# Second channel layer in seven block products for some rounds, and a new order at the seams between batches

## The chip, the cores and the metric

One core of a Trainium2 chip. The metric is the device time of one execution in microseconds (us), taken as the median over runs. A core has a matrix engine (TensorE, PE in the profile, with its weight loads listed apart as PEld), a vector engine (VectorE, DVE), a scalar engine (ScalarE, ACT), a general engine (GpSimd, POOL) and a sync engine that issues transfers (SyncE, SP). Each engine works through its own queue of instructions in order, and waits at an instruction until what it needs is there. All data are 32-bit floats in on-chip memory (SBUF, 128 partitions); TensorE writes to a small accumulator memory (PSUM), from which VectorE and ScalarE read.

## The reference

Block-sparse attention, its output laid out as B x S x 512, then a block of a Fourier mix, a normalization and two channel layers. B = 4, H = 8, S = 768, D = 64, w_ch1 is 512 x 2048 and w_ch2 2048 x 512.

```python
scores = np.where(mask, q @ k.T / sqrt(D), -1e9)          # mask: blocks of 32 x 32
attn = softmax(scores) @ v                                # (B, H, S, D) -> x: (B, S, H*D)
...
mixed = np.real(fft(fft(x, axis=1), axis=2))
u = x + mixed
un = (u - mean(u)) / sqrt(var(u) + 1e-6)                  # along the last axis
out = u + np.maximum(un @ w_ch1, 0.0) @ w_ch2
```

## The kernel before

**Attention.** The heads of a batch go in four pairs. A unit is 128 keys by 384 queries of a pair; a slot is two units, a pair has six slots and a batch 24. For a unit TensorE makes the scores s (`scores`, L578), ScalarE their exponentials (`weigh`), and TensorE the values o (`values`, L652). The block mask comes in one of two ways. Where a unit is in `by_pe`, TensorE adds a large negative number to the masked scores by a product of two small bf16 `factors` (L588), and ScalarE writes the exponentials straight to a tile e (L598). Else ScalarE exponentiates in place (L606) and VectorE multiplies with a 0/1 mask (L608). Sums over the keys are gathered on POOL (`gather`, L638), or on VectorE (L633). Tiles e come from a pool `ep` of four.

**Placing.** A finished half of a pair's values, oT, is put into x (two tiles, xA and xB, for the halves of the sequence; each has two buffers, so batch b writes where batch b-2 was and has to wait until that one is stored). `place` turns oT on TensorE (xt, L675) and copies it by ScalarE (L676). For later pairs `place_blocks` (L686) does it by 16 transfers of 12 KB each, SBUF to SBUF (L691).

**Mixer.** It runs on x of batch b while the attention of the next batches goes on. `norm_steps` scales x by the reciprocal sums (L761); fold steps (128x1536, L784), along steps and across steps (pq, L887 on) make the Fourier mix; arrive and spread add it to x and take its statistics; `whiten` (L951) makes un. In batches 0 to 2 un is turned by blocks on VectorE and through DRAM (`un_blocks` L1010, far<-un; `un_back` L1020, unT<-far, eight transfers); in the last by TensorE (utp, L992).

**Channel layers.** The first layer is `quad` (L1077): two 128-wide blocks of its outputs by seven block products in place of eight (Strassen's way with fewer sums), each 2 matmuls of 128x384. What they need are sums of blocks of unT (`right`, L1052) and of weights (`left`, L1065 to L1072). VectorE adds the products up (L1095), ScalarE does the relu (L1099). The second layer is `channels` (L1142): for one half and one block m of 128 tokens, four matmuls of 128x512 (L1146) and an add into x (L1149). A round r is quads 2r and 2r+1 and then six calls of `channels`; a batch has four rounds, after the last of which x is stored (`store`, L1157). The last batch's second layer (`outputs`) is already in seven block products of four 128x256 matmuls (L1211).

**Order.** It is written out when the program is built. `slot(sl)` issues a slot of attention. The mixer's steps wait in a queue `apart`, quads and channel calls in `late`, placings and sums of the attention in `short`. `gap` issues steps of `apart` and `short` that fit by reckoned clocks (`when`, one for each engine, and `state["ready"]`); `until(met)` issues channel steps, each with a gap behind it, until a condition holds, such as that a half of batch b-2 is stored (`finished`). `begin(b)` starts a mixer, and from its last step on (`go`) units are masked by VectorE. Constants reckon waits: `BACK` is the time until unT is back, `LEAVES` the time from the last store's issue until x is free. At a seam, where batch b-2 has to be stored ahead of the placing of the first pair of batch b, `slot` calls `until` and then puts the placing into `short`, due after `LEAVES`.

Of the kernel before, what the change touches and what calls it, by code (L numbers as in the profile page):

```python
# [99 lines left out]
def kernel(  # L100
# [14 lines left out]
    nc = tc.nc  # L115
# [61 lines left out]
    ep = ctx.enter_context(tc.tile_pool(name="ep", bufs=4))  # L177
    acc_p = ctx.enter_context(tc.tile_pool(name="acc_p", bufs=2))
    sum_p = ctx.enter_context(tc.tile_pool(name="sum_p", bufs=1))
    big = ctx.enter_context(tc.tile_pool(name="big", bufs=1))  # L180
    tr_p = ctx.enter_context(tc.tile_pool(name="tr_p", bufs=2))
    zc_p = ctx.enter_context(tc.tile_pool(name="zc_p", bufs=1))
# [502 lines left out]

    def place_blocks(n, half):  # L686
        b, j = pairs[n]
        oT = o_of.pop((n, half)).rearrange("p (c t d) -> p c t d", t=P // BLK, d=BLK)
        for g in range(P // BLK):
            for t in range(P // BLK):  # L690
                nc.sync.dma_start(  # L691
                    out=x_of[b, half][BLK * t:BLK * t + BLK, :, j * P + BLK * g:j * P + BLK * (g + 1)],
                    in_=oT[BLK * g:BLK * g + BLK, :, t, :])

    def into_sums(key, j, sp):
        if j == 0:
# [281 lines left out]
    def mixer(b, xA, xB):  # L978
# [34 lines left out]
        def un_back():  # L1013

            for half in range(2):
                unT[half] = tr_p.tile([P, ND, T * P], FP32, tag="tr", name="unT")
                of = lines[half].rearrange("m (g j) (k a i) -> a j k (m g) i",
                                           j=BLK, a=P // BLK, i=BLK)
                for a in range(P // BLK):
                    nc.sync.dma_start(  # L1020
                        out=unT[half][BLK * a:BLK * a + BLK].rearrange(
                            "j k (g i) -> j k g i", i=BLK),
                        in_=of[a])
            state["back"] = max(when["PE"], state["ready"]) + BACK[b > 0]

        t, s = {}, {}
        K1, K2 = slice(0, ND // 2), slice(ND // 2, ND)
# [49 lines left out]
        def quad(p):  # L1077

            g = p // 2 % 2 if last else 0
            if p % 2 == 0:  # L1080
                for i in range(2):
                    hs[g, i] = room((2, 0)[g] + i, [P, 4, HS], "h" + "AB"[i])
            l1, l2 = 2 * (p % 2), 2 * (p % 2) + 1
            h11, h12, h21, h22 = (hs[g, i][:, l, :] for l in (l1, l2) for i in range(2))
            a11, a12, s2, a22 = blocks(p)
            b11, b21, b22 = unT[0][:, K1, :], unT[0][:, K2, :], unT[1][:, K2, :]

            def product(to, a, c, after=0.0):
                for k in range(ND // 2):
                    nc.tensor.matmul(to, a[:, k, :], c[:, k, :], start=(k == 0),  # L1090
                                     stop=(k == ND // 2 - 1))
                return busy("PE", PRODUCT, after) + HOP

            def plus(to, ps, a, at):
                tt(out=to, in0=ps, in1=a, op=ALU.add)  # L1095
                return busy("DVE", SUM, at) + HOP

            def relu(h, at):
                nc.scalar.activation(out=h, in_=h, func=ACT.Relu)  # L1099
                busy("ACT", RELU, at)  # L1100

            def combine(j):
                left(p + 1, j)
                busy("DVE", COMBINE)

            x, at = ps_m.tile([P, 512], FP32, tag="m", name="xp")[:, 0:HS], bank("m")
            z5, z7 = (ps_s.tile([P, 2, 512], FP32, tag="s", name=name)[:, 0, 0:HS]
                      for name in ("z5", "z7"))
            done = product(x, a11, b11)
            nc.scalar.copy(out=h11, in_=x)  # L1110
            p1 = busy("ACT", RELU, done) + HOP
            give(at, p1 - HOP)
            y, at = ps_m.tile([P, 512], FP32, tag="m", name="yp")[:, 0:HS], bank("m")
            p2 = product(y, a12, b21)
            done = product(z7, s2, t[2])
            u2 = plus(h21, z7, h11, max(done, p1))
            c11 = plus(h11, y, h11, p2)
            relu(h11, c11)
            done = product(z5, s[1], t[1])
            plus(h12, z5, h21, done)  # L1120
            combine(1)
            done = product(z7, s[3], t[3], u2)
            u3 = plus(h21, z7, h21, done)
            c22 = plus(h22, z5, h21, done)
            z_at[0] = c22
            relu(h22, c22)
            combine(3)
            gap(0.0, 1.9)
            done = product(y, a22, t[4], c11)
            c21 = plus(h21, y, h21, done)  # L1130
            give(at, c21 - HOP)
            relu(h21, c21)
            gap(0.0, 1.9, "t")
            done = product(z7, s[4], b22, u3)
            z_at[1] = plus(h12, z7, h12, done)
            relu(h12, z_at[1])
            combine(4)
            if last:
                for j in ((1, 2), (3, 4))[p % 2]:
                    output_right(p // 4, j, p // 2 % 2)  # L1140

        def channels(r, half, m):  # L1142

            y, at = ps_m.tile([P, DM], FP32, tag="m", name="y"), bank("m")
            for l in range(4):
                nc.tensor.matmul(y, hs[0, half][:, l, m * P:(m + 1) * P], w2_sb[:, 4 * r + l, :],  # L1146
                                 start=(l == 0), stop=(l == 3))
            x = (xA, xB)[half]
            nc.vector.tensor_tensor(out=x[:, m, :], in0=y, in1=x[:, m, :], op=ALU.add)  # L1149
            give(at, busy("DVE", 0.7, busy("PE", 3.45) + HOP))  # L1150
            if r == NF // 4 - 1:
                store(half, m)

        def store(half, m, cols=slice(0, DM), queue=nc.sync):
            x = (xA, xB)[half]
            for p0, cnt, rows in _rows(out[b][:, cols], T * half + m):
                queue.dma_start(out=rows, in_=x[p0:p0 + cnt, m, cols])  # L1157
            if m == out_of[half][-1]:
                finished.add((b, half))

        last = b == B - 1
        OUT = (2, 0, 1)
        out_of = (OUT, OUT if last else (0, 1, 2))
# [111 lines left out]
        if not last:  # L1278
# [3 lines left out]
                              sp[1][1], wh[0][0], ft[0][0], sp[1][2], wh[1][1], ft[1][1],  # L1282
                              sp[1][0], wh[1][2], ft[1][2], wh[1][0], ft[1][0]]
            after = ([("-", un_back, 0.0, 0.0, 0.0)] + le +
                     [("b", lambda i=i: right(i, 0, 1, 2), 0.0, 0.0, 1.0) for i in (1, 2, 3, 4)])
        rest = []
        for r in range(2 if last else 0):
            rest += [(lambda p=p: quad(p), 7 * PRODUCT) for p in range(4 * r, 4 * r + 4)]
# [2 lines left out]
        for r in range(0 if last else NF // 4):  # L1291
# [9 lines left out]
    MOST, LEAST = 9.6, 2.5  # L1301
    COVER = 100.0
    AHEAD = 2.2
    BACK = 13.0, 12.0
    ALONE = 3.0
    LEAVES = 9.0
    SP = UP // SLOT
    SB = SP * NP
    W_PACE = 1.42
# [1 line left out]
    asked = set()  # L1311
    needed = set()
    state = {"paired": False, "total": None, "w": 0, "got": 0, "owed": 0.0, "ready": 0.0,
             "back": 0.0}

    def channel_step():
        late.popleft()[0]()

    def behind(kind):

        at = max(when["DVE"], state["ready"])
        return 0.75 * (len(kind) - 1) if when["POOL"] > at else 0.0

    def do_apart():
        kind, fn, pe, act, dve, _ = apart.popleft()
        if kind[0] in "dwb":
            dve += behind(kind)
            state["ready"] = busy("DVE", dve, {"w": rstd_at[0] if rstd_at else 0.0,
                                               "b": state["back"]}.get(kind, state["ready"])) + HOP
            fn()  # L1330
            return
# [10 lines left out]
            give(at, done - HOP)  # L1342
        state["ready"] = done

    def gap(rest=0.0, ahead=None, kinds="tm"):

        used = "".join(k for k in "tm" if k not in kinds)
        if ahead is None:
# [1 line left out]
        while apart:  # L1350
# [3 lines left out]
            if kind[0] in "dwb":  # L1354
                dve += behind(kind)
                if kind in "wb" and (state["back"] if kind == "b" else rstd_at[0]) > max(
                        when["DVE"], when["PE"]) + 0.2:
                    break
                if max(when["DVE"], state["ready"]) + dve > when["PE"] + rest + ahead:
                    break  # L1360
            elif kind != "-":
                bank_at = max(min(free[k]) for k in kind)
# [9 lines left out]
                short.remove(item)  # L1372
                fn()

    def until(met):

        while not met():
            if late:
                channel_step()
                gap(2.0)  # L1380
            else:
                do_apart()

    def begin(b):

# [6 lines left out]

        def go():
            late.extend(rest)
            masks["by_pe"] = False
        apart.append(("-", go, 0.0, 0.0, 0.0, hold))

    def rest():
# [19 lines left out]
    def slot(sl):  # L1418
# [28 lines left out]
            keep_mask = mask_step(2 * (sl // 3 - 1) + sl % 3 // 2)  # L1447
        for u, ps in got:
            weigh(u, ps)
        if keep_mask:  # L1450
            keep_mask()
        if BY_VECTOR <= n + 1 < len(pairs):
# [12 lines left out]
        if s == 0 and 0 < n < len(pairs) - 1:  # L1465
            load_k(n + 1)

        reuse = n % NP == 0 and phase >= 2
        if s >= (5 if reuse else 3) and (n, 0) in oT_at and once(n):
            b, j = pairs[n]  # L1470
            at = oT_at[n, 0]
            if reuse:
                until(lambda: (b - 2, 0) in finished)
                at = when["PE"] + LEAVES
            if in_blocks(n):
                place_blocks(n, 0)
            else:
                short.append(("t", at, lambda: place(n, 0)))
# [44 lines left out]
        for _ in range(4 if phase > 1 and not late and len(apart) < 6 * T else 0):  # L1523
            if apart and not late and (apart[0][0] != "b" or
                                       state["back"] < max(when["DVE"], when["PE"]) + 0.2):
                do_apart()

        must = (3, 5) if paired else (2, 5)
        soon = r == 0 and all(i[1] < when["PE"] + 1.0 for i in short)
# [47 lines left out]
        if sl == B * SB - 2:  # L1577
            over = nc.values_load(flag[0:1, 0:1], min_val=0, max_val=1)
    begin(B - 1)
    until(lambda: len(finished) == 2 * B)  # L1580
    ordered.close()


# [102 lines left out]
```

## Time and profile before

| | |
|---|---|
| runs, median (lowest to highest) | 1059.56 us (1056.76 to 1062.27), 3 runs |
| the profiled execution | 1059.17 us, of which the span 1057.5 us |
| TensorE clock, mean over the span | 0.993 of full |
| TensorE: s L578, o L652 | 155.2 us, 142.7 us |
| TensorE: y L1146 (hB, hA) | 129.2 us, 127.9 us |
| TensorE: z L1090 by unT, t | 93.1 us |
| POOL: sums of attention L638 | 163.6 + 47.1 us |

The span is the time between the first and last instruction of the profiled execution. A group in the profile is named by line, engine, operation and its tiles: out<-in. Busy times of groups on TensorE overlap at their ends, since matmuls are pipelined. Two instructions appear in the trace for each 32-bit matmul (two passes). Idle time is given with its releaser: the instruction whose end let the waiting one go.

### The profile page before, as it was taken

How to read it: one execution, taken by the hardware profiler on the slowest of the kernel's cores; microseconds unless marked ns; L12 is line 12 of the kernel's file. 1: busy time of each engine (PE TensorE's matmuls, PEld its weight loads, DVE VectorE, ACT ScalarE, POOL GpSimd, SP SyncE). 2: the span in 40 equal slices, each digit the busy share in tenths (PEclk: the TensorE clock that was granted, in tenths of full speed). 3: DMA queues.
4: the chain of work that ended last, by engine and by line, in shares of the span. 5: the costliest groups of instructions: out<-in, count | busy, mean ns of one | idle time of the engine just before them, and what ended most of it. 6: DMA issues, size and time to landing. Idle time of an engine off the chain costs nothing.

```text
span 1057.5 us, 12421 instructions
## 1 busy us (share of the span) xinstructions
PE 1022.8 (97%) x4338; PEld 530.7 (50%) x4338; DVE 675.3 (64%) x1235; ACT 356.2 (34%) x718; POOL 240.2 (23%) x270
## 2 busy tenths in 40 slices
PE   8989999997999999999999999899999999999996
PEld 4434345433465553444444654444444654578585
DVE  5899795968745744564578467565457364674663
ACT  6988755562020111342441212153220211210210
POOL 1000183565000100454553001256520001000000
PEclk9999999999999999999999999999999999999998
DMA  7757422292000124212230003821000001000001
GB/s 210 228 177 227 107 47 46 50 140 36 1 0 21 40 30 76 62 32 50 41 56 1 1 10 93 107 39 27 11 11 6 0 1 38 23 1 1 1 17 46
DMA packets 160385, 55.71 MB, mean 53 GB/s; under 512 B 145708, under 2 KB 151098, under 8 KB 160314
## 3 DMA queue, kind: packets, MB, share of 16 engines
q1 hardware_dynamic: 159062, 54.10, 23.9%
q10 hardware_dynamic: 1220, 0.72, 0.3%
q8 instruction: 36, 0.59, 0.2%
q14 instruction: 35, 0.29, 0.1%
q0 software_dynamic: 32, 0.01, 0.0%
HBM read 41.44 MB, written 11.01 MB: 50 GB/s over the span
## 4 chain that ended last, share of the span: by engine, by line
PE 82%; DVE 8%; ACT 3%; DMA 3%; issue 2%; SPq 1%; ACTq 0%; DVEq 0%
PE y L1146 23%; PE z L1090 15%; PE s L578 10%; PE o L652 9%; PE yp L1090 7%; PE yy L1211 7%; PE xp L1090 4%; PE zp L856 2%; ACT e L598 1%; DMA out_dram<-x 1%; PE sp L719 1%; PE s L588 1%; DVE t L1052 1%; DVE x L926 1%; DVE acc L633 1%
## 5 line engine op out<-in xcount | busy, mean ns | idle before, releaser
L638 POOL TENSOR_TENSOR acc<-acc,e 128x384 f32<-128x384 f32 x162 | 163.6, 1046 | 103.8 <-DVE e L608 84.5
L578 PE MATMUL s<-qT,kT 64*128 64x384 f32 x768 | 155.2, 518 | 13.0 <-DVE e L608 6.5
L652 PE MATMUL o<-e,vr 128*64 128x384 f32 x768 | 142.7, 499 | 0.0
L1146 PE MATMUL y<-w_sb,hB 128*128 128x512 f32 x288 | 129.2, 600 | 0.3 <-DVE x L1149 0.3
L1146 PE MATMUL y<-w_sb,hA 128*128 128x512 f32 x288 | 127.9, 595 | 0.0
L1149 DVE TENSOR_TENSOR x<-y,x 128x512 f32<-128x512 f32 x72 | 49.7, 691 | 119.9 <-PE y L1146 119.8
L608 DVE TENSOR_TENSOR e<-s,mask 128x768 f32<-128x768 f32 x90 | 82.0, 951 | 54.9 <-ACT s L606 47.6
L578 PEld LDWEIGHTS s<-qT,kT 64*128 64x128 f32 x768 | 63.8, 186 | 92.3 <-ACT e L598 25.2
L638 POOL TENSOR_TENSOR acc<-e 128x384 f32<-128x384 f32 x42 | 47.1, 1143 | 254.5 <-ACT e L598 124.6
L606 ACT ACTIVATE s<-s 128x768 f32<-128x768 f32 x90 | 68.4, 792 | 89.4 <-PE s L578 89.1
L1090 PE MATMUL z<-unT,t 128*128 128x384 f32 x256 | 93.1, 486 | 2.0 <-DVE hA L1095 2.0
L598 ACT ACTIVATE e<-s 128x768 f32<-128x768 f32 x102 | 77.7, 811 | 48.5 <-PE s L588 32.0
L1146 PEld LDWEIGHTS y<-w_sb,hB 128*128 128x128 f32 x288 | 53.9, 192 | 67.6 <-issue 65.8
L1146 PEld LDWEIGHTS y<-w_sb,hA 128*128 128x128 f32 x288 | 53.7, 190 | 63.7 <-issue 60.2
L652 PEld LDWEIGHTS o<-e,vr 128*64 128x64 f32 x768 | 48.2, 137 | 71.6 <-issue 68.7
L1095 DVE TENSOR_TENSOR hA<-z,hA 128x384 f32<-128x384 f32 x64 | 35.7, 558 | 69.8 <-PE z L1090 69.6
L1099 ACT ACTIVATE hA<-hA 128x384 f32<-128x384 f32 x64 | 33.5, 523 | 129.3 <-DVE hA L1095 129.3
L1090 PEld LDWEIGHTS z<-unT,t 128*128 128x128 f32 x256 | 48.6, 190 | 36.8 <-DVE hA L1095 3.1
L1099 ACT ACTIVATE hB<-hB 128x384 f32<-128x384 f32 x64 | 33.5, 523 | 86.6 <-DVE hB L1095 86.6
L1110 ACT COPY hA<-xp 128x384 f32<-128x384 f32 x32 | 15.3, 478 | 116.0 <-PE xp L1090 116.0
L1090 PE MATMUL z<-t,w_sb 128*128 128x384 f32 x128 | 46.9, 489 | 5.0 <-DVE e L608 3.4
L1090 PE MATMUL z<-t,t 128*128 128x384 f32 x128 | 47.8, 497 | 0.0
(208 smaller groups left out, 1367.0 us busy)
## 6 DMA issues: line engine op xcount, KB each, us to landing
wraw<-in_moe_w_ch_dram SPq DMA_DIRECT2D x32, 512.0 KB
vr<-in_v_dram SPq DMA_DIRECT2D x30, 192.0 KB
far<-un SPq DMA_DIRECT2D x18, 256.0 KB
unT<-far SPq DMA_DIRECT2D x24, 192.0 KB
qb<-in_q_dram SPq DMA_DIRECT2D x44, 96.0 KB
kb<-in_k_dram SPq DMA_DIRECT2D x44, 96.0 KB
x<-oT SPq DMA_DIRECT2D x192, 12.0 KB
out_dram<-x SPq DMA_DIRECT2D x11, 252.0 KB
```

The lines of the kernel that those rows point to most:

```text
L578: nc.tensor.matmul(s[:, i, 0:HS], kT[rows, c * P:(c + 1) * P], qT[rows, queries], start=True, stop=u not in by_pe)
L598: nc.scalar.activation(out=e, in_=s[:, :, 0:HS], func=ACT.Exp, scale=scale)
L606: nc.scalar.activation(out=s[:, :, 0:HS], in_=s[:, :, 0:HS], func=ACT.Exp, scale=scale)
L608: nc.vector.tensor_tensor(out=e, in0=s[:, :, 0:HS], in1=m.broadcast_to([P, 2, HS]), op=ALU.mult)
L638: nc.gpsimd.tensor_add(out=acc[:, i, :], in0=start[:, i, :], in1=e[:, i, :])
L652: nc.tensor.matmul(o[D * i:D * i + D, :], vt[:, i, c, :], e[:, i, :], start=(c == 0), stop=(c == C - 1))
L1090: nc.tensor.matmul(to, a[:, k, :], c[:, k, :], start=(k == 0), stop=(k == ND // 2 - 1))
L1095: tt(out=to, in0=ps, in1=a, op=ALU.add)
L1099: nc.scalar.activation(out=h, in_=h, func=ACT.Relu)
L1146: nc.tensor.matmul(y, hs[0, half][:, l, m * P:(m + 1) * P], w2_sb[:, 4 * r + l, :], start=(l == 0), stop=(l == 3))
L1149: nc.vector.tensor_tensor(out=x[:, m, :], in0=y, in1=x[:, m, :], op=ALU.add)
L1211: nc.tensor.matmul(ps, a[:, k, :], c[k // 2][:, k % 2, :] if isinstance(c, list) else c[:, k, :], start=(k == 0), stop=(k == 3))
```

## The change

1. **Rounds in seven products.** Where a quad with an even number is issued while `until` runs with `alone` set, and the round isn't the batch's last, the round's second layer goes by `round_of`: for each m, one 2 x 2 product of blocks (token halves by halves of the round's hidden units, and these by halves of the 512 outputs) in seven products of two matmuls of 128x256. In the order as built these are five rounds: 0, 1 and 2 of batch 0, 2 of batch 1 and 2 of batch 2. The sums of weights are made by POOL (`round_right`), those of hidden values by VectorE (1 and 2) and POOL (3 and 4) (`round_left`). Products go into x by VectorE from PSUM (`plus`, and `both` for two at once), or are copied out by ScalarE (`keep`) and added by POOL (`later`). The sums' room is the four e tiles and a new one; `drain` first issues the values that still need e.
2. **Placing by blocks** goes through DRAM: four transfers out and four back in place of 16.
3. **Seams.** The first placing of a pair that reuses x is issued behind the exponentials of the next slot, not when due by `LEAVES`. `until` runs one slot earlier there if there are late steps, `LEAVES` is 13 (9), `BACK` of batch 2 is 15 (12), the rights of batch 0 are reckoned at 1.7 (1.0), POOL's hindrance (`behind`) at 0.25 in rounds alone (0.75). Masking by VectorE starts with the first channel step, not with `go`. A pending total is issued once the batch before is stored, ahead of a mixer step on PSUM. `gap` can be given a start (`start`) by which alone steps on VectorE are let in. A half counts as stored after three full stores. The last `until` runs with `alone`.

The diff, cut to its core:

```diff
     def place_blocks(n, half):
         b, j = pairs[n]
-        oT = o_of.pop((n, half)).rearrange("p (c t d) -> p c t d", t=P // BLK, d=BLK)
+        rows = far_p.tile([BLK, T, P // BLK, P], FP32, tag=f"oT{half}", name="row", bufs=2)
+        oT = o_of.pop((n, half))
         for g in range(P // BLK):
-            for t in range(P // BLK):
-                nc.sync.dma_start(
-                    out=x_of[b, half][BLK * t:BLK * t + BLK, :, j * P + BLK * g:j * P + BLK * (g + 1)],
-                    in_=oT[BLK * g:BLK * g + BLK, :, t, :])
+            nc.sync.dma_start(
+                out=rows.rearrange("r c t f -> r (c t) f")[:, :, BLK * g:BLK * g + BLK],
+                in_=oT[BLK * g:BLK * g + BLK, :].rearrange("r (ct d) -> r ct d", d=BLK))
+        for t in range(P // BLK):
+            nc.sync.dma_start(
+                out=x_of[b, half][BLK * t:BLK * t + BLK, :, j * P:(j + 1) * P],
+                in_=rows[:, :, t, :])
...
+            if not last:
+                if p % 2 == 0:
+                    seven[p // 2] = state["alone"] and p // 2 < NF // 4 - 1
+                elif seven[p // 2]:
+                    state["drain"]()
+                    sums_room()
+                    for j in (1, 2, 4, 3):
+                        round_right(p // 2, j)
...
+        def round_right(r, j):
+            a, c = {1: (part(r, 0, 1), part(r, 0, 0)), 2: (part(r, 1, 1), w_t[1]),
+                    3: (part(r, 1, 1), part(r, 0, 1)), 4: (part(r, 1, 0), w_t[2])}[j]
+            nc.gpsimd.tensor_tensor(out=w_t[j], in0=a, in1=c, op=ALU.subtract)
...
+        def round_left(m, j):
+            a11, a12, a21, a22 = tokens(m)
+            to, a, c, op = {1: (h_s[1], a21, a22, ALU.add), 2: (a21, h_s[1], a11, ALU.subtract),
+                            3: (h_s[3], a22, a21, ALU.subtract),
+                            4: (h_s[4], a12, a21, ALU.subtract)}[j]
+            if j > 2:
+                nc.gpsimd.tensor_tensor(out=to, in0=a, in1=c, op=op)
...
+            else:
+                tt(out=to, in0=a, in1=c, op=op)
...
+            if m == OUT[0]:
+                round_left(m, 1)
+                round_left(m, 2)
+            c_at, at = ps_m.tile([P, 512], FP32, tag="m", name="yc")[:, 0:DH], bank("m")
+            a_at = plus(a0, c_at, product(c_at, a12, part(r, 1, 0), True))
+            give(at, a_at - HOP)
+            k0 = keep(0, u_at, product(u_at, a11, part(r, 0, 0), True, z_at[0]))
+            later(a0, 0, max(a_at, k0))
+            o_at, at = ps_m.tile([P, 512], FP32, tag="m", name="yc")[:, 0:DH], bank("m")
+            give(at, plus(b0, o_at, product(o_at, a22, w_t[4], True)) - HOP)
+            if m == OUT[0]:
+                round_left(m, 3)
+                round_left(m, 4)
+            gap(start=0.9)
+            k1 = keep(1, u_at, product(u_at, a21, w_t[2], False, k0))
+            later(a1, 1, k1)
+            k2 = keep(2, d_at, product(d_at, h_s[1], w_t[1], True, z_at[1]))
+            done = product(u_at, h_s[3], w_t[3], False, k1)
+            tt(out=both, in0=both,
+               in1=u_at.rearrange("p (o d) -> p o d", o=1).broadcast_to([P, 2, DH]), op=ALU.add)
+            z_at[0] = busy("DVE", 0.7, done) + HOP
+            later(b1, 2, max(z_at[0], k2))
+            z_at[1] = plus(a1, d_at, product(d_at, h_s[4], part(r, 1, 1), False, k2))
+            ahead(1, 2, 3, 4)
+            state["soon"] = 1.6
...
             after = ([("-", un_back, 0.0, 0.0, 0.0)] + le +
-                     [("b", lambda i=i: right(i, 0, 1, 2), 0.0, 0.0, 1.0) for i in (1, 2, 3, 4)])
+                     [("b", lambda i=i: right(i, 0, 1, 2), 0.0, 0.0, 1.0 if b else 1.7)
+                      for i in (1, 2, 3, 4)])
...
     def channel_step():
+        masks["by_pe"] = False
         late.popleft()[0]()
...
     def do_apart():
         kind, fn, pe, act, dve, _ = apart.popleft()
+        if finished and kind[0] in "mt" and state["total"] in short:
+            short.remove(state["total"])
+            state["total"][2]()
...
-                if max(when["DVE"], state["ready"]) + dve > when["PE"] + rest + ahead:
+                at = max(when["DVE"], state["ready"]) - when["PE"]
+                if at + dve > rest + ahead if start is None else at > start:
                     break
...
         for u, ps in got:
             weigh(u, ps)
+        if state["place"]:
+            state["place"]()
+            state["place"] = None
...
-        if s >= (5 if reuse else 3) and (n, 0) in oT_at and once(n):
+        if s >= ((4 if late else 5) if reuse else 3) and (n, 0) in oT_at and once(n):
             b, j = pairs[n]
             at = oT_at[n, 0]
             if reuse:
-                until(lambda: (b - 2, 0) in finished)
-                at = when["PE"] + LEAVES
-            if in_blocks(n):
+                until(lambda: (b - 2, 0) in finished, s == 4)
+                state["place"] = lambda: place(n, 0)
+            elif in_blocks(n):
                 place_blocks(n, 0)
```

Beside `round_of`, `plus` is a VectorE add of 128x256 from PSUM into x, `keep` a ScalarE copy of 128x256 out of PSUM, `later` a POOL add of it into x, `ahead` the lefts of the next m.

## The prediction

> **What bounds the kernel now.** First the page's busy rows, the tenths by slice and the granted clock, then the chain that ended last: is one engine the limit, and everywhere?
>
> ```profile
> PE 1022.8 (97%) x4338; PEld 530.7 (50%) x4338; DVE 675.3 (64%) x1235; ACT 356.2 (34%) x718; POOL 240.2 (23%) x270
> ...
> PE   8989999997999999999999999899999999999996
> ...
> PEclk9999999999999999999999999999999999999998
> ...
> PE 82%; DVE 8%; ACT 3%; DMA 3%; issue 2%; SPq 1%; ACTq 0%; DVEq 0%
> ```
>
> TensorE is busy for 1022.8 of 1057.5 us, so time can come from two places only: fewer passes through it, or the 34.7 us in which it stands. The slices below 9 tell where it stands; the stretches there, with the clock in the third column from the right, are these (us, then busy time and count of PE, PEld, DVE, ACT, POOL; clock; DMA share; GB/s):
>
> ```profile
> 234.00:262.00 28.00, 22.65 (x91) 10.32 (x87) 22.92 (x29) 11.21 (x24) 15.30 (x14) 0.94 0.45 53
> 260.00:400.00 140.00, 140.00 (x428) 75.96 (x427) 81.96 (x168) 23.36 (x51) 11.84 (x20) 1.00 0.11 20
> 405.60:420.00 14.40, 12.44 (x49) 4.87 (x51) 8.18 (x10) 4.68 (x8) 0.00 (x0) 0.88 0.35 73
> 672.00:695.00 23.00, 17.71 (x72) 8.18 (x72) 13.12 (x19) 7.04 (x17) 5.50 (x7) 0.93 0.37 80
> ```
>
> In the channel rounds alone (260 to 400) TensorE never stands. At the three seams, where a batch's rounds begin or end, it loses 5.35, 1.96 and 5.29 us and some clock besides: 28 x 0.06 = 1.7, 14.4 x 0.12 = 1.7, 23 x 0.07 = 1.6 us. Its timeline says behind what (brackets: idle before, and what ended it):
>
> ```profile
> 245.19 1.61 PE L1090 MATMUL z<-t,w_sb 128*128 128x384 f32 x4 [3.36 <-DVE e L608]
> ...
> 251.35 1.56 PE L1090 MATMUL z<-unT,t 128*128 128x384 f32 x4 [1.99 <-DVE hA L1095]
> ...
> 412.73 2.35 PE L578 MATMUL s<-qT,kT 64*128 64x384 f32 x8 [1.96 <-DVE e L608]
> ...
> 674.43 1.53 PE L1090 MATMUL z<-t,w_sb 128*128 128x384 f32 x4 [1.58 <-DVE t L1052]
> ...
> 689.37 2.50 PE L578 MATMUL s<-qT,kT 64*128 64x384 f32 x8 [3.71 <-DVE e L608]
> ```
>
> And why the exponentials' products (e, L608) were late is in ScalarE's timeline:
>
> ```profile
> 410.51 0.48 ACT L676 COPY x<-xt 128x384 f32<-128x384 f32 x1 [13.10 <-DMA out_dram<-x]
> 410.88 1.50 ACT L606 ACTIVATE s<-s 128x768 f32<-128x768 f32 x2
> ...
> 687.09 0.48 ACT L676 COPY x<-xt 128x384 f32<-128x384 f32 x1 [4.82 <-DMA out_dram<-x]
> 687.46 1.50 ACT L606 ACTIVATE s<-s 128x768 f32<-128x768 f32 x2
> ```
>
> The placing copy (L676) needs x free, so it waits for the store of two batches earlier, and the exponentials stand in ScalarE's queue behind it.
>
> **The rounds.** Pass prices come from two runs of equal passes:
>
> ```profile
> 564.78 10.46 PE L1146 MATMUL y<-w_sb,hB 128*128 128x512 f32 x24
> 575.08 1.45 PE L1090 MATMUL xp<-unT,w_sb 128*128 128x384 f32 x4
> ...
> 945.45 3.62 PE L1211 MATMUL yy<-ot,os 128*128 128x256 f32 x16
> 948.90 1.89 PE L1211 MATMUL yy<-w_sb,os 128*128 128x256 f32 x8
> ```
>
> 24 passes of 512 columns take 575.08 - 564.78 = 10.30, 0.429 each; 16 of 256 take 948.90 - 945.45 = 3.45, 0.2156 each. A matmul is two passes. A round was 48 x 0.429 = 20.60; as seven products of two matmuls for each of three blocks it is 84 x 0.2156 = 18.11. Gain 2.49; five rounds **-12.45**. Weight loads (190 ns in group L1146) stay under 215.6.
>
> What else a round costs. VectorE: six adds of 0.69 go; in come six lefts and nine adds of 128x256 (0.42 each, as L1218 and L1072 show) and three adds of 128x512 (0.69): 8.4 for 4.1 in 18.1 us. ScalarE: nine 128x256 copies, 0.38 each by a 128x257 one. Both fit. POOL has no 128x256 row; its 128x384 add takes 0.965 alone (four in 3.87 at 440.53) and 1.23 beside VectorE (eight in 9.83 at 233.62), hence an estimate of 0.64 to 0.82, and 1.29 to 1.64 for 128x512. The four factors of weights (5.2 to 6.6) lie under the second quad (7 products, about 9 us). In the block, one product is 4 x 0.2156 = 0.86. VectorE's second left is ready some 2.2 after the start, needed at 2.59. POOL's lefts 3 and 4 stand behind its first add: ready at 4.2 to 4.5 and 4.9 to 5.3, needed at 4.31 and 5.17: 0 to 0.5 lost in each first block; later blocks have theirs made ahead, 0 to 0.3. Bounds 0 to 8 (the upper under the second rival); I take **+2.0**, nearer the lower, since VectorE is free for some 10 us of a round.
>
> Here a rule speaks against the change. Row: a VectorE 128x768 subtract of two SBUF operands takes 0.95 at 406.87 with POOL idle and up to 1.75 at 240.86 beside it. The Trainium skill, "SBUF — State Buffer", section "Who interferes with whom", says such an instruction and a GpSimd one that reads SBUF exclude each other, the second blocked wholly. The trace agrees in part: 1.75 is less than 0.95 plus a whole 1.23. By it the sum becomes the second rival's.
>
> Four more units are masked on TensorE (L588): 4 passes take 186.94 - 186.52 = 0.42 a slot, two slots **+0.84**.
>
> **Seam A (238 to 252).** The first quad's products wait because the mask products (L608) and four slow rights (1.63 to 1.75 each) share VectorE. After, both slots before the quad are masked on TensorE, so their exponentials need no VectorE, and the quad starts near 242 rather than 245. The five x<-x,r (4.43 from 246.40), which made the 1.99, start later, since a total is taken early and steps are spread. -(5.35 + 1.7) + 0.5 left = **-6.55** (bounds -7.05 to 0).
>
> **Seam B (405 to 420).** The placing is issued behind the next slot's exponentials, so they no longer wait for the store; transposes and copy stand behind them, needed only by later mixer steps. -(1.96 + 1.7) + 0.5 = **-3.2** (-3.7 to 0).
>
> **Seam C (655 to 695).** The same for 3.71, and stores now go out before the unT loads on SP's queue, which made both copy and rights late; but eight unT transfers (issued 657 to 668, landed near 672) still come under 6 us before their use. I leave 2.0: -(1.58 + 3.71 + 1.6) + 2.0 = **-4.9** (-6.9 to 0).
>
> **Seam D (876 to 905).** The last batch's first rounds now start with the across steps behind them: after p8 VectorE has about 10 us of steps before the next transposes, with 20 us of TensorE work as cover, but utp and the first z follow in one run. Idle there was 0.35 + 0.80 + 0.25 = 1.4; by my layout 3.4: **+2.0** (0 to +4).
>
> **Attention behind B and C** runs 7 to 8 slots without channel work in place of 4. A slot is 2.83 us on TensorE, and POOL's sums 2 units x 5/6 x 1.93 = 3.22: 0.4 a slot for up to seven slots, 0 to 2.7 each; the first slots have slack in the e tiles: **+1.5**.
>
> **Placing by blocks**: 16 transfers cost SP 10.32 us (445.35); after, 4 + 4 with a landing between, 2.6 + 2.8 (a store's DMA) + 2.6 = 8. SP's next are loads a pair ahead; the one consumer that waited (x, L761, 3.1 us) is hidden by TensorE work. **0** (-1 to +3, the 3.1 if the cover is gone).
>
> The changed reckonings (BACK, LEAVES, `right`, `behind`) and the count of stores issue nothing; they shift steps, and what that does is in the terms of the seams.
>
> **Sum**: -12.45 + 2.0 + 0.84 - 6.55 - 3.2 - 4.9 + 2.0 + 1.5 = -20.8; 1059.17 - 20.8 = **1038**. The profiled 1059.17 (span 1057.5, 1.67 around it) is 0.4 under the median 1059.56, which I neglect.
>
> **Rivals.**
>
> 1. *The seams' waits come back at the rights.* Seams A and C have a second releaser, the rights (L1052) and, for C, the landing of unT; exponentials that are early gain nothing there. Back come 3.36 + 1.7 at A and 1.58 + 1.71 + 1.6 at C: 1038 + 10 = **1048**. For it: t L1052 ended the 1.58. Against: at A the rights end at 244.2 only because mask products and POOL's eight sums lie beside them. Chance 0.18.
> 2. *POOL shuts out VectorE in the rounds.* Each of the first two lefts waits for a whole POOL instruction, 0.75: 2.2 + 1.5 - 2.59 = 1.1 in five first blocks, 0.3 in ten later ones, 8.5 in place of 2.0: **1045**. For it: 1.75 beside 0.95. Against: adds with a PSUM operand (hA L1095) take 0.56 either way. Chance 0.13.
> 3. *Slower: long mixer steps queued on VectorE between a round's adds.* In the three rounds of batch 0 they are there: sa and sd folds (128x1536, L784, 1.75 to 1.85 alone; x 1.75/0.95 beside POOL = 3.2). A block gives 0.8 of slack, so each such step stops TensorE for 2.4, as the adds hold the two PSUM tiles that the next block opens with. In all 15 blocks 36 us in place of 2: 1038 + 34 = **1072**. It decides from (20.8 + 2)/15 = 1.5 us a block. Against: the trace has eight such folds in all, and x<-x,r at 0.89 fits the slack. Chance 0.12.
> 4. *No new waits at all*: without the terms +2.0, +2.0, +1.5 and the 3.0 left at the seams, **1030**. Chance 0.07.
>
> That the rounds aren't split where they are said to be is not a rival: seven products are chosen while a batch's rounds run alone, which is known when the program is laid out.
>
> **How the numbers follow.** Forecast 0.50 (own range 1033 to 1044), rivals 0.18, 0.13, 0.12, 0.07. No change means within 0.5% of 1059.56, 1054.3 to 1064.9, about what a measurement can tell. Faster: 0.50 + 0.07, 0.15 of rival 1, 0.11 of rival 2 = 0.83. Same: 0.03 + 0.02 + 0.03 of rival 3 = 0.08. Slower: the 0.09 left of rival 3. The range goes from rival 4, 1030, to 1055, past rivals 1 and 2 with the upper bounds of D and of the attention stretches (+2 and +4).
>
> **What would show it.** Rounds: 14 passes of 256 columns in a row start 0.216 apart, with under 0.5 us idle in a first block; waits there for POOL's lefts speak for my term, for VectorE's lefts for rival 2, for x adds behind folds for rival 3. Seam A: no idle over 1 us at the first z; B: L606 ahead of L676 in ScalarE's timeline and no dip in the clock; C: idle of at most 2 in all. A sum under 1055 with idle left at L1052 is rival 1. The forecast is wrong if TensorE stands more than 25 us in all or its passes are slower than 0.22.

## The result, and the profile after

| | median of runs (lowest to highest) | profiled span | clock |
|---|---|---|---|
| before | 1059.47 us (1056.71 to 1062.27), 20 runs | 1057.5 us | 0.993 |
| after | 1061.2 us (1059.8 to 1063.49), 20 runs | 1060.2 us | 0.986 |

The ratio is 1.0022, with a 95% interval of 1.0013 to 1.0030: a little slower, where 1038 us was forecast. Some 23 us of expected gain are missing. The page after, in the same rows:

```profile
PE 1014.9 (96%) x4526; PEld 564.1 (53%) x4526; DVE 712.8 (67%) x1292; ACT 373.2 (35%) x763; POOL 327.3 (31%) x363
...
PE   8999999999999999799999999869999999999996
...
PEclk9999999999999999899999999989999999999998
```

TensorE works 7.9 us less, but stands 45.3 us (1060.2 - 1014.9) in place of 34.7, and runs longer at a low clock. The low digits have moved. The slice at 240 is full now: the first seam is mended. The lows at 424 and 690 are new ones. In the stretches behind the second and third seam:

```profile
420.00:440.00 20.00, 12.69 (x67) 4.69 (x67) 13.88 (x16) 8.44 (x13) 13.79 (x14) 0.98 0.91 128
440.00:460.00 20.00, 19.85 (x74) 9.58 (x76) 12.73 (x19) 6.93 (x16) 7.71 (x8) 0.85 0.32 70
...
680.00:700.00 20.00, 10.30 (x54) 3.98 (x54) 12.48 (x15) 6.72 (x11) 11.37 (x13) 0.80 0.76 113
700.00:720.00 20.00, 20.00 (x84) 9.15 (x80) 10.89 (x19) 8.13 (x18) 8.37 (x9) 0.95 0.18 43
```

First the rounds, from TensorE's timeline (products of the first round of batch 0, and the quad behind it):

```profile
263.23 1.03 PE L1211 MATMUL yc<-w_sb,hA 128*128 128x256 f32 x4
264.09 1.03 PE L1211 MATMUL yz<-w_sb,hA 128*128 128x256 f32 x4
...
267.92 1.13 PE L1211 MATMUL yz<-of 128*128 128x256 f32 x4 [0.21 <-POOL of L1193]
...
281.84 1.45 PE L1103 MATMUL xp<-unT,w_sb 128*128 128x384 f32 x4
```

A product takes 0.86, a pass 0.215, as priced. The round is over in 281.84 - 263.23 = 18.61, for 18.11 without a wait. The wait is at the place expected, for POOL's left 3 in a first block; line L1211 waited 2.0 us in all, four times. So the rounds themselves are done in the time forecast. Then the second seam (TensorE, and with it VectorE, ScalarE and SyncE):

```profile
419.90 1.78 PE L579 MATMUL s<-qT,kT 64*128 64x384 f32 x8 [1.68 <-DVE e L609]
420.49 11.31 SPq L1025 DMA_DIRECT2D unT<-far  x8
...
429.48 1.78 PE L579 MATMUL s<-qT,kT 64*128 64x384 f32 x8 [1.29 <-DVE e L609]
...
431.90 3.03 SPq L231 DMA_DIRECT2D qb<-in_q_dram  x4
...
435.54 0.96 DVE L1057 TENSOR_TENSOR t<-unT 128x768 f32<-128x768 f32 x1 [5.26 <-DMA unT<-far]
...
438.21 0.84 ACT L536 ACTIVATE qT<-qb 128x768 f32<-128x768 f32 x1 [6.12 <-DMA qb<-in_q_dram]
...
439.14 1.81 DVE L609 TENSOR_TENSOR e<-s,mask 128x768 f32<-128x768 f32 x2
440.15 2.93 PE L579 MATMUL s<-qT,kT 64*128 64x384 f32 x8 [6.17 <-DVE e L609]
```

In the profile before, the eight unT<-far were issued from 389.50 to 400.17, under channel work, 17 us before that attention:

```profile
389.50 10.67 SPq L1020 DMA_DIRECT2D unT<-far  x8
400.27 7.81 SPq L1157 DMA_DIRECT2D out_dram<-x  x7
...
406.48 1.56 PE L578 MATMUL s<-qT,kT 64*128 64x384 f32 x8
```

Now they come at 420.49, in the middle of it, and hold SyncE's queue for 11.3 us. The load of q behind them comes late and ScalarE waits 6.12 for it; VectorE waits 5.26 for unT with the mask products queued behind its rights; TensorE stands 6.17 us. The third seam repeats it with a longer wait, this time with the placing in it (VectorE may write oT only when the transfers row<-oT, behind unT and q on SyncE, have read the last one):

```profile
673.69 11.10 SPq L1025 DMA_DIRECT2D unT<-far  x8
...
684.89 3.54 SPq L231 DMA_DIRECT2D qb<-in_q_dram  x4
...
688.53 2.74 SPq L692 DMA_DIRECT2D row<-oT  x4
...
692.86 0.58 DVE L661 STREAM_TRANSPOSE oT<-o 128x384 f32<-128x384 f32 x1 [5.57 <-DMA row<-oT]
...
697.93 2.93 PE L579 MATMUL s<-qT,kT 64*128 64x384 f32 x8 [8.40 <-DVE e L609]
```

### The profile page after: what moved, and what is told of

It reads as the page before. It is cut to its first block, busy times and chain, and to the rows that moved or that the text cites. A ratio compares the mean times of both kernels' runs of the same rounds, so it can differ in the third digit from the quotient of the medians.

```text
span 1060.2 us, 13059 instructions
## 1 busy us (share of the span) xinstructions
PE 1014.9 (96%) x4526; PEld 564.1 (53%) x4526; DVE 712.8 (67%) x1292; ACT 373.2 (35%) x763; POOL 327.3 (31%) x363
## 4 chain that ended last, share of the span: by engine, by line
PE 82%; DVE 7%; ACT 3%; POOL 2%; DMA 2%; issue 2%; SPq 2%; DVEq 0%; ACTq 0%; POOLq 0%
PE z L1103 16%; PE y L1268 12%; PE s L579 10%; PE o L653 8%; PE yp L1103 8%; PE yy L1336 7%; PE xp L1103 4%; PE yz L1211 3%; PE yw L1211 2%; PE yc L1211 2%; PE zp L861 2%; DVE e L609 1%; POOL acc L639 1%; PE s L589 1%; ACT e L599 1%
## 5 line engine op out<-in xcount | busy, mean ns | idle before, releaser
L579 PE MATMUL s<-qT,kT 64*128 64x384 f32 x768 | 157.6, 525 | 28.8 <-DVE e L609 22.3
L609 DVE TENSOR_TENSOR e<-s,mask 128x768 f32<-128x768 f32 x86 | 78.3, 948 | 36.7 <-ACT s L607 31.1
L599 ACT ACTIVATE e<-s 128x768 f32<-128x768 f32 x106 | 80.9, 811 | 53.3 <-PE s L589 34.9
L1108 DVE TENSOR_TENSOR hA<-z,hA 128x384 f32<-128x384 f32 x64 | 35.6, 556 | 67.0 <-PE z L1103 66.9
L1268 PE MATMUL y<-w_sb,hB 128*128 128x512 f32 x168 | 75.2, 596 | 0.0
L1268 PE MATMUL y<-w_sb,hA 128*128 128x512 f32 x168 | 75.1, 595 | 0.0
L1224 POOL TENSOR_TENSOR x<-of,x 128x256 f32<-128x256 f32 x45 | 34.8, 780 | 125.2 <-ACT of L1216 85.2
L1271 DVE TENSOR_TENSOR x<-y,x 128x512 f32<-128x512 f32 x42 | 28.9, 688 | 54.8 <-PE y L1268 54.8
L1268 PEld LDWEIGHTS y<-w_sb,hB 128*128 128x128 f32 x168 | 31.1, 190 | 38.8 <-issue 38.6
L1268 PEld LDWEIGHTS y<-w_sb,hA 128*128 128x128 f32 x168 | 31.1, 190 | 37.3 <-issue 36.0
L1103 PE MATMUL xp<-unT,w_sb 128*128 128x384 f32 x128 | 49.9, 515 | 0.0
L1103 PE MATMUL yp<-unT,w_sb 128*128 128x384 f32 x128 | 47.4, 493 | 0.0
```

Source lines behind the costliest of these rows:

```text
L579: nc.tensor.matmul(s[:, i, 0:HS], kT[rows, c * P:(c + 1) * P], qT[rows, queries], start=True, stop=u not in by_pe)
L599: nc.scalar.activation(out=e, in_=s[:, :, 0:HS], func=ACT.Exp, scale=scale)
L609: nc.vector.tensor_tensor(out=e, in0=s[:, :, 0:HS], in1=m.broadcast_to([P, 2, HS]), op=ALU.mult)
```

## The experiments

All ratios are against the kernel before, on the same chip, with a 95% interval. Diffs are against the changed kernel unless another is named. Where two variants are set beside each other by their medians, they may come from different chips; the kernel before differed by 1.6 us between these sets of runs (1058.41 to 1059.97), so differences near 1 us say nothing.

**Which half gains?**

```diff
-                    seven[p // 2] = state["alone"] and p // 2 < NF // 4 - 1
+                    seven[p // 2] = False
```

> All of the change, but no round goes by seven products. Theory M (the seven-product rounds hold the next batch's mixer steps on VectorE back, so that unT comes back after the seam, and its eight transfers and the rights stall the attention): unT<-far is issued before the last stores again, the idle times of 6.17 and 8.40 us and the clock lost behind them (20 x 0.15 = 3.0, 20 x 0.20 + 20 x 0.05 = 5.0) go but for some 4, the five rounds give back 12.5: 1061.2 + 12.5 - 22.6 + 4 = 1055. Rival S (the new order at the seams makes these waits by itself): both stay, 1061.2 + 12.5 = 1074.

Measured: 1044.95 us, 0.9871 (0.9845 to 0.9896). Without the rounds the change gains 15 us, 10 more than my theory M gave this run. Of the waits at the seams only one over 0.6 is left, 1.31; TensorE's waits, added up over the timeline's brackets, are 13.9 us, against 24.3 before and 35.1 after (some 10 us of the 34.7 and 45.3 above stand in no bracket). The five rounds, worth 12.45, cost 16.

From here on the mixer's steps are followed in time. The rounds of batch 0 lie beside the mixer of batch 1 (us from the span's start, from the timelines):

| | before | seams_only | after |
|---|---|---|---|
| last x<-x,r ends | 257 | 267 | 278 |
| first product of the across steps (pq) | 314 | 310 | 353 |
| last whitening (un<-x,st) ends | 364 | 362 | 418 |
| unT<-far issued from | 390 | 382 | 420 |
| first store of batch 0 issued | 400 | 393 | 387 |

With the rounds the mixer is 38 to 56 us behind from the across steps on, though the channel work beside it is 6 us ahead.

**Is it the place of each round?** Conditions on batch and round in place of `p // 2 < NF // 4 - 1`:

```diff
+ three_rounds:   p // 2 < NF // 4 - 1 and b == 0
+ one_round:      (b, p // 2) == (1, 2)
+ two_rounds:     (b, p // 2) in ((0, 2), (2, 2))
+ three_rounds_2: (b, p // 2) in ((0, 1), (0, 2), (2, 2))
+ last_round:     (b, p // 2) == (2, 2)
```

> All of the change, but only the three rounds of batch 0 by seven products, not round 2 of batches 1 and 2. Theory M: the stall behind batch 0's rounds (6.17) stays, that behind batch 1's (8.40 and 5.0 of clock) goes but for 2; two rounds give back 5.0: 1061.2 + 5.0 - 11.4 = 1055. Rival S: both stay, 1066.

1051.39 us, 0.9931 (0.9904 to 0.9957). The third seam's 8.40 is gone, the second keeps 4.79.

> All of the change, but by seven products only round 2 of batch 1, which in the order as built puts unT's return behind the stores at the third seam. Theory M: 1044.95 - 2.5 + the stall behind batch 1's rounds (8.40 idle, 5.0 clock, less the 1.3 that is there without it, some 12) = 1055. Rival Q: 1048.

1054.92 us, 0.9958 (0.9944 to 0.9973), as theory M has it: a single round in batch 1 costs 10 us, with unT issued at 666.2 (646.4 without) and 8.16 us idle at 690.24.

> All of the change, but by seven products only round 2 of batch 0 and round 2 of batch 2, where in the order as built unT is issued back before the last stores at both seams. Theory M (a seven-product round costs by holding the next batch's mixer back until unT returns behind the seam, and gains 2.5 us where it doesn't): 1044.95 - 2 x 2.5 = 1040, no idle over 2 us at the seams. Rival Q (each such round costs by itself, the five cost 1061.2 - 1044.95 = 16.3, so 3.3 each): 1051.5.

1048.66 us, 0.9897 (0.9873 to 0.9921). A miss: here unT returns before the stores, only 6.5 us later than in seams_only (388.7 for 382.2), and yet TensorE stands 5.41 us at 412.31.

> All of the change, but by seven products only rounds 1 and 2 of batch 0 and round 2 of batch 2; unT's return at the second seam lies among the stores in the order as built. Theory M: 1044.95 - 7.5 + 0 to 4 at the second seam (more_steps, with unT at the same place, stood 1.87 + 1.30 there) = 1037 to 1042. Rival Q: 1055.

1051.47 us, 0.9922 (0.9899 to 0.9946). A miss too: 11.70 us idle at 415.79. The last stores stand behind unT's eight issues (395.87 to 408.15), ScalarE's placing copy waits 14.59 us for them, and the next exponentials stand behind the copy.

> All of the change, but by seven products only round 2 of batch 2, behind which no unT comes back through memory. Theory M: the round's 2.5 us are gained, 0.7 to 1.1 lost at the last mixer's first transposes: 1044.95 - 2.5 + 0.9 = 1043. Rival Q (each such round costs by itself): 1046 or more.

1043.17 us, 0.9853 (0.9837 to 0.9870). The round of batch 2, behind which the last mixer turns un on TensorE and sends nothing through memory, gains about what it was priced at: 1.8 us against seams_only, of 2.5 less some 0.9 forecast. This is the fastest version of the study, 18 us under the changed kernel. Rival Q, a cost of each round by itself, is out for this round.

**Is it the rule by which steps are let in, or the rounds' own work?** gaps_only against seams_only, more_steps against the changed kernel:

```diff
+ gaps_only (in channels):   if state["alone"] and r < NF // 4 - 1:
+                                state["soon"] = (0.9, 1.6)[half]
- more_steps (in round_of):  state["soon"] = 1.6
+                            state["soon"] = 3.6
```

> No round by seven products, but mixer steps are let in behind a channel call by the rounds' rule (until VectorE is reckoned 0.9 or 1.6 us ahead). If the rule by itself holds the mixer back as far as the rounds do: unT returns behind the seams and stalls come back, 1055 to 1067. If it is the rounds' own work on VectorE and POOL: within 3 us of seams_only, 1045.

1077.3 us, 1.0166 (1.0142 to 1.0190). Without one product of a round, the rounds' rule alone holds the mixer back: the across steps begin at 333 (310 in seams_only), unT is issued at 403 (382) and, in the next batch, at 697 (646), and 10.95 us are lost there in one wait. How much of the rounds' effect this is, the run doesn't say. Beside the rounds of batch 0 the rule brings 21 of the 38 us by which unT is late, and no wait over 1.30 us at the second seam. In batch 1 it also works behind the calls that the change leaves in eight products, and there it holds the mixer back more than the rounds do (across steps from 626, 606 after), which may be why this run is slower than the changed kernel.

> All of the change, all five rounds, one number changed: after a block of a seven-product round, mixer steps on VectorE are let in until it is reckoned 3.6 us ahead of TensorE, not 1.6. Theory M: unT is back before the seams' end, both stalls go but for some 4: 1061.2 - 22.6 + 4 = 1043, with no idle over 3 us after the seams. Rival S: the stalls stay, 1061. Rival P (the steps stand in the way of the rounds' adds): the seams' stalls go, but the 15 blocks lose about 1 us each, 1058.

1061.95 us, 1.0025 (1.0009 to 1.0040). With more steps let in, unT is issued at 405 and 654 and not 420 and 674, but 3.13 us go in a quad behind mixer steps (hA L1108), and 1.87, 3.68 and 5.20 at the seams. The time is that of the changed kernel; neither M nor P fits alone. My reading, which no run tests, is that behind the sum of the rounds' and the mixer's steps there is less slack than a reckoning of VectorE's busy time shows.

**What makes the attention wait?** First the rights. BACK for batches 1 and 2, in two_rounds and in the changed kernel:

```diff
- two_rounds_18: BACK = 13.0, 12.0, 15.0
+                BACK = 13.0, 18.0, 15.0
- rights_later:  BACK = 13.0, 12.0, 15.0
+                BACK = 13.0, 16.0, 19.0
```

> two_rounds with BACK = 18 in place of 12 for batch 1: the only difference in the order is that at the second seam the four rights stand two slots of masks and an add later on VectorE. Theory M2 (rights that wait for unT's transfers keep the mask products behind them, and with these TensorE): the 5.41 us at 412 and the clock lost there (20 x 0.17 = 3.4) go, 1048.7 - 8.8 = 1040. Rival L (the attention would wait for late loads or stores there anyway): 1046 to 1049.

1048.52 us, 0.9900 (0.9883 to 0.9916).

> All of the change with all five rounds, BACK = 13, 16, 19 in place of 13, 12, 15: at the second and third seam the rights stand one or two mask products later, unT's issue and all loads stay where they are. Theory M2: the waits of 6.17 and 8.40 us fall to what VectorE's transposes into oT and ScalarE's squares of q still wait for SP's queue, some 3 each: 1061.2 - 8.6 - 4 of clock = 1049. Rival L (SP's queue, held 11 us by unT's issues, stops q's load and the placing, and these stop the attention whatever the rights do): 1058 to 1061.

1061.63 us, 1.0019 (1.0002 to 1.0036). Theory M2 falls: with the rights away in two_rounds_18 the wait is 5.16 us for 5.41. rights_later says less, since the wait moves and the four rights still stand between it and the mask product. There TensorE stands 8.21 us at 445.22, as ScalarE's squares of q wait 6.27 and VectorE's oT waits 5.38 for transfers that SyncE issued behind unT. In two_rounds_18 SyncE and ScalarE show what is behind the 5.16 us:

```profile
388.74 9.96 SPq L1025 DMA_DIRECT2D unT<-far  x8
...
398.82 8.87 SPq L1279 DMA_DIRECT2D out_dram<-x  x10
...
409.04 0.48 ACT L677 COPY x<-xt 128x384 f32<-128x384 f32 x1 [8.05 <-DMA out_dram<-x]
...
410.25 1.50 ACT L607 ACTIVATE s<-s 128x768 f32<-128x768 f32 x2
...
412.09 2.93 PE L579 MATMUL s<-qT,kT 64*128 64x384 f32 x8 [5.16 <-DVE e L609]
```

The stores stand behind unT's issues. The placing copy waits 8.05 for them, and the next slot's exponentials behind the copy: the chain of the kernel before at this seam, one slot later. So SyncE's queue was tested from both sides. (`queue` stands for what issues unT<-far in batches 1 and 2.)

```diff
+ two_unback_pool:   two_rounds, queue = nc.gpsimd
+ two_unback_half:   two_rounds, queue = nc.scalar if a % 2 else nc.sync
+ after_unback_pool: queue = nc.gpsimd
+ seams_held:        seams_only, and behind the eight unT<-far:
+                    for a in range(P // BLK):          # for each half
+                        nc.sync.dma_start(out=more[BLK * a:BLK * a + BLK]..., in_=of[a])
```

> seams_only, but SyncE issues each unT<-far of batches 1 and 2 a second time, into memory that nobody reads. Theory SP: its queue is held 10 us longer, the stores at the second seam go out 10 us later and a wait like two_rounds' comes, at the third seam kb and the last stores too: 1044.95 + 8 to 14 = 1053 to 1059. If the queue isn't the cause: 1045 to 1047.

1063.02 us, 1.0037 (1.0022 to 1.0053). Nothing but issues on SyncE is added, and the gain of 15 us is gone:

```profile
382.03 10.22 SPq L1025 DMA_DIRECT2D unT<-far  x8
392.30 11.19 SPq L1035 DMA_DIRECT2D more<-far  x8
403.59 9.22 SPq L1289 DMA_DIRECT2D out_dram<-x  x10
...
414.08 0.48 ACT L677 COPY x<-xt 128x384 f32<-128x384 f32 x1 [12.94 <-DMA out_dram<-x]
```

TensorE then stands 8.82 us at 417.20, and 5.12 at the third seam. The transfers load the memory as well, so issue and traffic are not told apart by this run alone.

> two_rounds, but POOL's queue issues the eight unT<-far of batches 1 and 2. Theory SP (SyncE's queue, held 10 us by these issues, delays the stores, and so the copy and the exponentials behind it): the 5.41 us and some 3 of clock go, 1048.7 - 8 = 1041. Rival T (the transfers themselves land late, or load the memory, whoever issues them): 1047 to 1050.

1046.39 us, 0.9885 (0.9855 to 0.9916). The copy runs at 403.83, 5 us sooner, and the wait falls from 5.41 to 3.08; what is left is unT's landing, at 403.04, with the masks behind the rights. Theory SP has 2.3 of the 8 us it gave. Nor is the queue all that changed: from 380 to 412 us the profile has unT's 1.57 MB in 512 packets on POOL's queue, and 905 packets under 512 bytes in all, where two_rounds has 12,953.

> two_rounds, but ScalarE's queue issues four of the eight unT<-far of batches 1 and 2. Theory SP: SyncE's queue is free 5 us earlier, the wait falls from 5.4 to under 1: 1042, plus up to 2 for relus behind ScalarE's issues: 1042 to 1044. Rival T: 1047 to 1051.

1055.81 us, 0.9970 (0.9957 to 0.9983). Slower by 7, and at the second seam, where theory SP expected under 1 us, TensorE still stands 4.92:

```profile
388.05 6.77 SPq L1025 DMA_DIRECT2D unT<-far  x4
394.93 14.80 SPq L1279 DMA_DIRECT2D out_dram<-x  x10
...
408.10 0.48 ACT L677 COPY x<-xt 128x384 f32<-128x384 f32 x1 [7.81 <-DMA out_dram<-x]
...
411.16 2.93 PE L579 MATMUL s<-qT,kT 64*128 64x384 f32 x8 [4.92 <-DVE e L609]
```

SyncE begins the stores 3.95 us sooner than in two_rounds (394.93 for 398.88), but the first of them takes 2.64 us to issue, for 0.77 there, and the copy that waits for the stores runs only 1.15 us sooner (408.10 for 409.25). So the hold of SyncE's queue is not the whole cause here; the traffic of the transfers is left as a rival, and no run changes the one without the other. At the third seam ScalarE's own exponentials stand behind the four transfers that it issues (6.80 us from 649.44), and TensorE stands 6.12 us.

> All of the change with its five rounds, but POOL's queue issues the eight unT<-far of batches 1 and 2. Theory SP: q's load and the placings come 11 us earlier, the waits of 6.17 and 8.40 fall to the landing of unT for the rights, some 3 to 5 each, with the clock: 1061.2 - 12 = 1049; POOL's sums behind its issues may give back a few. Rival T: 1058 to 1066.

1078.58 us, 1.0180 (1.0142 to 1.0217). Slower by 17: POOL's issues wait 7.84 us for the last far<-un, the attention's sums stand behind them, and VectorE's mask product waits 11.08 for a sum, as it needs the e tile. On each queue that was tried, something of the attention stood behind these transfers; in seams_only, where SyncE takes them under channel work, only one wait over 0.6 us, of 1.31, is left at the seams.

**What gained the 15 us?** Parts of the seams' edits undone in seams_only, and one in the changed kernel:

```diff
+ place_old:       short.append(("t", when["PE"] + LEAVES, ...)), LEAVES = 9, BACK 12 for batch 2
+ seams_place_old: the same in seams_only
+ seams_s5:        seams_place_old, and s >= (5 if reuse else 3)
+ seams_mask_old:  seams_only, masks["by_pe"] = False in go() again
```

> All of the change, but at a seam the first placing is put into the queue of short steps again, due by LEAVES = 9, and BACK is 12 again for batch 2. Theory M: neither moves unT's return, both stalls stay within 2 us, 1060 to 1064. Rival S (placing behind the exponentials makes the waits): both go, 1047.

1059.51 us, 1.0001 (0.9986 to 1.0015): both stalls stay (6.23 and 6.74), so the new place of the placing did not make them.

> seams_only with the first placing of a seam in the queue of short steps again, due by LEAVES = 9, BACK 12 for batch 2. If placing behind the exponentials is what removed the waits for the stores (1.96 and 3.71 us and 3.3 of clock): 1044.95 + 9 = 1054. If one slot earlier and the masks did it: 1045 to 1047.

1046.14 us, 0.9881 (0.9864 to 0.9897). It is worth 1.2 us at most, which is within the spread between the sets of runs, not 9.

> seams_place_old (placing in the queue of short steps, LEAVES 9), and the channel steps at a seam run from the sixth slot of the pair again, not the fifth. If the slot earlier removed the waits behind the stores (1.96 and 3.71 and 3.3 of clock): 1046.1 + 9 = 1055. If it didn't: 1045 to 1047.

1050.96 us, 0.9931 (0.9914 to 0.9947). The slot earlier is worth 4.8: without it 3.00 us stand at 680.66 and 1.18 at the first seam. About half of what was forecast for it.

> seams_only, but units are masked by VectorE from the mixer's last step on again, not from the first channel step. If masking by TensorE is what cleared the first seam, its waits (5.35 us and 1.7 of clock, less 0.4 of TensorE's mask passes) come back: 1044.95 + 6.6 = 1051.6. If the other edits there did it: 1044 to 1046.

1045.26 us, 0.9875 (0.9859 to 0.9892). A wait of 1.36 behind mask products is back at 246.76, the mask passes are saved, and the sum is 0.3. The masks did not clear the first seam. Of the 15 us some 6.3 are found at most (1.2 + 4.8 + 0.3); the rest is not found. The reckonings for rights and POOL, the early total and the placing by eight transfers were not undone one by one. In seams_only x<-x,r begins at 253.6 and not at 246.4, so the 1.99 us behind five of these is gone with their new place.

## Why the prediction was wrong

- **Pass price and waits in the rounds: right.** 0.215 a pass, 18.61 for a first round, 2.0 us of waits in all where 2.0 was taken. POOL's adds of 128x256, an estimate of 0.64 to 0.82, took 0.78 in the mean (L1224), and last_round is 1.8 us faster than seams_only.
- **"VectorE: ... 8.4 for 4.1 in 18.1 us. ... Both fit": the step that failed.** VectorE's share does fit (the rounds' own steps took 43.0 us in five, 8.6 each); what was not costed is the work that the rounds are laid out beside. By the prediction's own figures VectorE had 20.6 - 4.1 = 16.5 us for other work beside a round before, and 18.1 - 8.4 = 9.7 after. The next batch's mixer goes through the gaps of the rounds in a fixed order, and it came late: its last product, unT, was sent for 17 us ahead of the attention at the second seam before, and at 420.49, amid the attention, after. That distance belonged in the sum and wasn't in it. At the third seam the term of seam C took the transfers at 657 to 668; they were issued from 673.69 to 684.79. The text said that the reckonings "issue nothing; they shift steps", and that the terms of the seams hold what this does; they hold no later unT. So eight transfers that hold SyncE's queue for 10 us lost their cover. Where the terms left 0.5 + 2.0 + 1.5 = 4.0 us at seams B and C and in the attention behind them, 22.3 of waits and 8.4 of clock came.
- **What is open in it.** That the rounds make the mixer late is shown (seams_only, one_round), and so is that a mixer made late without them costs time too (gaps_only). How the lateness divides between the rule of the gaps, the rounds' shorter cover and VectorE's slower steps is not, nor whether the hold of the queue or the traffic does the harm. Against seams_only the spans differ by 1060.2 - 1043.1 = 17.1; the rounds' -12.45, +21.2 of waits (35.1 - 13.9) and +9.2 of clock below full (15.2 - 6.0, summed over 20 us slices) make 18.0.
- **Seams: the sum was too small, the reasons half wrong.** 14.65 less what masks, D and attention add gave 10.3 without the rounds; 15 were measured. Placing behind the exponentials was priced at the whole of seam B and the 3.71 of C and is worth 1.2 at most, the masks at seam A 0.3. That 15 came out for 10.3 is in part luck.
- **Seam D** stood 1.16 + 0.73 for 0.80 + 0.35 before: half a microsecond or so, and a clock of 0.91 for 20 us, near the 2.0 taken.
- **Attention behind B and C**: small waits of 0.90, 1.68 and 1.29 came at each seam, 7.8 in place of 1.5, above the bound of 5.4; in the 1.68 VectorE had late steps of the mixer (un L956, L1015) ahead of the mask products.
- **Rivals.** The first named unT's landing and the rights, at 10 us; it is the nearest, but gave the rights the blame, and moving them gained nothing. The second (POOL shuts out VectorE) shows in no wait of TensorE, but it does in VectorE's steps: x<-x,r took 23.0 us in all and x<-x,un 25.6, for 18.5 and 21.0 in seams_only, which is part of the mixer's lateness. The third had the right engines, VectorE's queue and the mixer, and the wrong victim: the mixer waits for the rounds, not the rounds for the mixer.

## What to carry to other kernels

Where an engine at 97% is relieved, ask first what the time that goes was covering. Here the channel work covered a chain of another batch (VectorE steps, a trip through memory, eight transfers that hold a queue for 10 us), and a shorter cover with fewer gaps moved that chain into a stretch that can't bear it. Follow the last step of such a chain by its time of issue, before and after, as one of the terms; and put a faster stage first where nothing that is woven into it has to be back through memory at a seam, as last_round does.

## What the runs showed of the hardware

Issuing holds the queue that does it: the eight unT<-far of 192 KB, in runs of 128 bytes, held SyncE's for 9.96 (two_rounds_18) to 12.28 us (three_rounds_2), 1.25 to 1.5 each, and what stood behind them in that queue waited. The time is not the queue's alone: with four on SyncE and four on ScalarE at once (two_unback_half) each took 1.6 to 1.7 on either (6.77 and 6.45; 6.80), and on POOL four took 3.96.

Around the longest waits the granted clock fell over a 20 us slice: to 0.85 behind the 6.17 us and 0.80 around the 8.40 in the changed kernel, to 0.74 around 8.16 in one_round. Shorter waits went both ways (the Trainium skill, "TensorE: Matmul & The Clock Gate", "Part 1: The HAM clock gate", has the clock halved after an idle window of about 3.4 us; 3.00 us in seams_s5 and 1.68 and 1.29 at the second seam of the changed kernel left it at 1.00, which agrees, while 1.96 us before the change went with 0.88, which doesn't). The same two waits at the last mixer's start, 1.16 and 0.73 us, went with 0.91 in the changed kernel and with 1.00 in last_round, so the length of a wait alone doesn't tell.
